# Order and size of the load bursts of a cached attention block, and half of its normalisation on another engine

## The chip, the cores and the metric

The kernel runs on one core of one Trainium2 chip. The metric is the device time of one execution in microseconds (us); lower is better. The kernel before took 459.73 us, the median of three runs (453.28 to 465.25).

A core has five engines that run their own instruction streams and meet only through semaphores: TensorE (matmuls; in the profile PE, with its weight loads as PEld), VectorE (DVE), ScalarE (ACT), GpSimd (POOL) and SyncE (SP), which here only issues transfers. Sixteen DMA engines carry out the transfers. Operands live in SBUF, matmul results in PSUM.

## The reference

```python
# x [8,112,640]; k_cache, v_cache [8,32,512,192]; wq [640,6144]; wo [6144,640]; all bf16
q = (x @ wq).reshape(B, Sq, H, Dh).transpose(0, 2, 1, 3)
scores = einsum("bhqd,bhkd->bhqk", q, k_cache) * Dh ** -0.5
p = softmax(scores, axis=-1)
o = einsum("bhqk,bhkd->bhqd", p, v_cache)
return o.transpose(0, 2, 1, 3).reshape(B, Sq, H * Dh) @ wo
```

Eight batches of 112 queries attend with 32 heads to 512 cached keys and values of width 192. Each cache holds 50.3 MB, each weight matrix 7.9 MB; all of it is read once.

## The kernel before, in words

**Units.** The work is cut into 64 units: a unit is one batch and a group of four heads (`u = 8 * g + b`). Eight groups follow one another, and within a group the eight batches. For a unit, TensorE computes the scores transposed (S, 96 small matmuls), ScalarE takes their exponential (`exp`, L932), TensorE multiplies by V (PV, 16 matmuls; a column of ones beside V gives the row sums), VectorE normalises (`do_NM`, L976 to L986), TensorE transposes the result (T, 6 matmuls), and ScalarE moves it to `oT` (`tevac`, L941). There is no maximum subtraction; the sums are instead checked for their range on GpSimd, and a flag would start a second, slower program that isn't run with these inputs.

**Projections.** The Q projection of a later group (`do_Q`) and the output projection of an earlier one (`do_O`) are cut into items, and `items_at[u]` spreads them over the units: mostly one Q item and two O items in a unit, in the third unit of a group four Q items and no O, in the fifth two Q items and two O. The items share two PSUM banks in turn, so an item waits for the eviction of the item before the last (`bank_free`).

**The order on each engine** is written out by hand. TensorE's pass u is S(u), PV(u-1), the first items, T(u-1), the other items. VectorE's pass is two of four transposes of K for unit u+2 (`do_KT`, L974, which also wait until S(u) has released their buffer), the normalisation of unit u-1, and the other two transposes among evictions of O items. ScalarE's pass is the four exponentials of unit u, the first Q evictions, `tevac(u-1)`, the other Q evictions.

**Normalisation.** `do_NM(u)` waits for PV(u); a reduction adds two partial sums a head (L979), a reciprocal follows (L982), a memset clears a column of PSUM for the next PV (L983), and one multiply of 112 x 768 values writes `os` (L986). T(u) waits for it (`vNM`). Heads 0 and 1 stand in one PSUM bank, heads 2 and 3 in the next.

**Loads.** K and V have four buffers each (`NK`, `NV`), filled by two halves of 384 KB; Wq and Wo have two buffers each, filled by pieces of 192 and 160 KB. SyncE issues all loads in one queue, in an order fixed when the program is built. A load waits on SyncE until its buffer is free: K for the transposes (`vKT`) of the unit four before, V for PV (`pPV`) of the unit four before, and everything behind it in the queue waits too.

**Periods.** TensorE's instructions are themselves fetched by DMA, in pieces of 16,384 bytes, as the records of the instruction queue show. `put` counts TensorE's instructions; at the first suitable matmul after each 256 of them, the first after 194 (`FIRST`), it raises `pF`. SyncE issues loads in bursts, one for each of the 69 periods so marked, each after a wait for `pF` (near L1125). Which loads belong to a burst is worked out from a nominal time: `place` is the unit that TensorE is in, plus a fraction. In the kernel before, each load has one number, the place at which it may be issued (K of u+3 at u, V of u+2 at u+0.5, and so on), the list is sorted by it, and a burst takes from its head whatever is at most 0.45 ahead of `place`, without a limit on bytes.

**The start.** Before the first period, SyncE issues the input, Wq of group 0, K(0), and after the first Q item K(1) and V(0).

## Time and profile before

| | |
|---|---|
| median of three runs | 459.73 us |
| the profiled execution's own time | 465.36 us |
| its span, first to last instruction | 463.7 us |
| mean granted TensorE clock | 0.971 |
| TensorE matmuls busy | 402.9 us, 87% |
| VectorE busy | 320.4 us, 69% |
| ScalarE busy | 220.1 us, 47% |
| data queue, share of 16 DMA engines | 80.0%, 118.71 MB |
| transposes of K, x256 | 870 ns each |
| exponentials, 448 wide, x256 | 550 ns each |
| multiply of the normalisation, x64 | 958 ns each |
| reciprocal, x64 | 178 ns each |
| K half-load, issue to landing, median | 5.2 us |
| V half-load, issue to landing, median | 5.0 us |

How to read it: the profile's page gives busy time by engine, forty slices of the span, and groups of instructions by line with what ended the idle time before them. Ends of matmuls are modelled, so a busy TensorE isn't necessarily one at its peak; its weight loads (PEld) show gaps more sharply. All TensorE instructions pass through a helper, so their lines are those of `matmul` (L800) and `transpose` (L803), and what they work on tells them apart: `qT,kt` is S, `vs,pT` is PV, `ident,os` is T, `xT,wqs` a Q item, `wos,oT` an O item. In the chain and the waits, `issue` is time in which the engine waited for nothing that the profile shows. The chain follows the work that ended last back from its end; the times there are when a step began and how long it held the chain.

### The profile page before, as it was taken

The page shows a single profiled execution, that of the slowest core. Times are in us where ns is not written, and L with a number is a line of the kernel's source. Part 1 is how long each engine was busy: PE and PEld are TensorE (multiplying, and loading weights), DVE is VectorE, ACT ScalarE, POOL GpSimd, SP SyncE. Part 2 cuts the span into 40 slices and gives each one's busy share as a digit, 9 for nine tenths or more (in the row PEclk, how much of TensorE's full clock was granted, in tenths as well). Part 3 has the DMA queues.
Part 4 walks back from the last instruction along what each step waited for, and adds up shares of the span by engine and source line. Part 5 has one row for each costly group of instructions (what it writes and reads, how often), then busy time and mean ns, then how long its engine had stood idle before and what let it go on. Part 6 is the DMA issues. An engine that isn't in the chain of part 4 may idle for free.

```text
span 463.7 us, 19950 instructions
## 1 busy us (share of the span) xinstructions
PE 402.9 (87%) x8749; PEld 303.9 (66%) x8749; DVE 320.4 (69%) x635; ACT 220.1 (47%) x421; POOL 43.1 (9%) x210
## 2 busy tenths in 40 slices
PE   8948997999889698999896999899878998897782
PEld 4626775777667576677674777677656776675561
DVE  2636786877777665877785688777757777887542
ACT  3625553555446433565453555464435653553420
POOL 1001001110011010110010111101101101111010
PEclk9979999999999988999998999999989999999998
DMA  8898998799988868879994899989878788987601
GB/s 281 279 331 259 307 307 267 246 316 300 308 271 270 252 177 296 271 222 308 306 319 151 251 310 324 291 247 296 274 233 255 237 263 280 284 245 238 216 31 35
DMA packets 100654, 120.04 MB, mean 259 GB/s; under 512 B 5585, under 2 KB 84177, under 8 KB 100561
## 3 DMA queue, kind: packets, MB, share of 16 engines
q1 hardware_dynamic: 100560, 118.71, 80.0%
q8 instruction: 70, 1.15, 1.0%
q14 instruction: 24, 0.19, 0.1%
HBM read 117.54 MB, written 1.15 MB: 256 GB/s over the span
## 4 chain that ended last, share of the span: by engine, by line
PE 48%; DMA 26%; DVE 12%; issue 9%; SPq 3%; ACT 1%; DVEq 0%
PE ps L800 43%; DMA kr<-in_k_cache_dram 26%; DVE kt L974 7%; PE ps L803 4%; DVE os L986 4%; SPq L1085 1%; SPq L1099 1%; SPq L1091 1%; ACT pT L932 1%; DVE rinv L982 1%; SPq L1078 0%; ACT oT L941 0%; DVE ps L983 0%; ACT xT L913 0%; DVE sm L979 0%
## 5 line engine op out<-in xcount | busy, mean ns | idle before, releaser
L974 DVE STREAM_TRANSPOSE kt<-kr 128x384 int32<-128x384 int32 x256 | 210.7, 870 | 95.5 <-DMA kr<-in_k_cache_dram 57.9
L932 ACT ACTIVATE pT<-ps 128x448 bf16<-128x448 f32 x256 | 118.5, 550 | 75.1 <-PE ps L800 75.1
L800 PE MATMUL ps<-vs,pT 128*128 128x193 bf16 x1024 | 100.3, 250 | 19.5 <-issue 15.9
L800 PE MATMUL ps<-wos,oT 128*128 128x320 bf16 x672 | 111.3, 304 | 3.5 <-issue 2.6
L800 PE MATMUL ps<-xT,wqs 128*128 128x448 bf16 x480 | 107.2, 361 | 1.8 <-ACT xT L913 0.8
L800 PEld LDWEIGHTS ps<-vs,pT 128*128 128x128 bf16 x1024 | 83.7, 98 | 27.2 <-issue 18.6
L800 PEld LDWEIGHTS ps<-qT,kt 32*128 32x128 bf16 x6144 | 77.7, 93 | 18.9 <-issue 14.8
L800 PE MATMUL ps<-qT,kt 32*128 32x112 bf16 x6144 | 87.8, 209 | 0.7 <-ACT qT L924 0.7
L924 ACT ACTIVATE qT<-ps 128x448 bf16<-128x448 f32 x96 | 52.1, 544 | 73.2 <-PE ps L800 72.7
L941 ACT ACTIVATE oT<-ps 128x672 bf16<-128x672 bf16 x64 | 46.7, 730 | 80.4 <-PE ps L803 80.4
L800 PEld LDWEIGHTS ps<-wos,oT 128*128 128x128 bf16 x672 | 64.0, 99 | 31.3 <-issue 4.2
L800 PEld LDWEIGHTS ps<-xT,wqs 128*128 128x128 bf16 x480 | 56.8, 126 | 26.0 <-issue 3.3
L986 DVE TENSOR_TENSOR os<-ps,rinv 112x768 bf16<-112x768 f32 x64 | 61.3, 958 | 2.2
L803 PE MATMUL ps<-ident,os 112*128 112x112 bf16 x384 | 30.9, 218 | 26.3 <-DVE os L986 26.0
L1062 POOL TENSOR_SCALAR bad<-rinv 112x4 f32<-112x4 f32 x64 | 14.4, 225 | 399.3 <-DVE rinv L982 399.3
L803 PEld LDWEIGHTS ps<-ident,os 112*128 112x128 bf16 x384 | 21.3, 100 | 44.0 <-DVE os L986 42.6
L1000 DVE TENSOR_TENSOR acc<-ps,acc 128x320 f32<-128x320 f32 x84 | 39.9, 475 | 2.4 <-PE ps L800 2.2
L979 DVE TENSOR_REDUCE sm<-ps 112x4 f32<-112x8 f32 x64 | 10.1, 158 | 23.4 <-PE ps L800 23.4
L1063 POOL TENSOR_SCALAR bad<-rinv 112x4 f32<-112x4 f32 x64 | 14.3, 224 | 4.0
L982 DVE RECIPROCAL rinv<-sm 112x4 f32<-112x4 f32 x64 | 11.4, 178 | 3.4
L1065 POOL TENSOR_TENSOR cnt<-cnt,bad 112x8 f32<-112x8 f32 x64 | 12.8, 200 | 5.3
L1000 DVE TENSOR_TENSOR xs<-ps,acc 128x320 bf16<-128x320 f32 x14 | 6.3, 482 | 2.2 <-PE ps L800 2.2
(30 smaller groups left out, 30.9 us busy)
## 6 DMA issues: line engine op xcount, KB each, us to landing
kr<-in_k_cache_dram SPq DMA_DIRECT2D x128, 384.0 KB, 5.2
vs<-in_v_cache_dram SPq DMA_DIRECT2D x128, 384.0 KB, 5.0
wos<-in_wo_dram SPq DMA_DIRECT2D x48, 160.0 KB, 5.2
wqs<-in_wq_dram SPq DMA_DIRECT2D x35, 192.0 KB, 4.4
out_dram<-xs SPq DMA_DIRECT2D x7, 160.0 KB, 2.6
wqs<-in_wq_dram SPq DMA_DIRECT2D x1, 960.0 KB
xs<-in_x_dram SPq DMA_DIRECT2D x1, 640.0 KB, 4.3
xs<-in_x_dram SPq DMA_DIRECT2D x1, 480.0 KB, 7.9
```

The lines of the kernel that those rows point to most:

```text
L800: return put(lambda: pe.matmul(out, w, m, start=start, stop=stop, **kw), start and not stop, us)
L803: return put(lambda: pe.transpose(out, m, eye), first, 0.05)
L924: act.activation(qT[g % 2][:, c, HQ * h:HQ * (h + 1)], ps[:, bank(it), 0:HQ], ACTF.Copy).then_inc(aQ, 1)
L932: act.activation(pT[u % 2][:, a, :, 0:SQ], ps[:, a, 0:4 * SQ].rearrange("p (t q) -> p t q", t=4), ACTF.Exp, scale=scale).then_inc(aEX, 1)
L941: act.activation(oT[:, :, SQ * b:SQ * (b + 1)].rearrange("p (k c) q -> p k c q", k=2), src.rearrange("p k (c q) -> p k c q", c=3), ACTF.Co ...
L974: dve.transpose(dst, src).then_inc(vKT, 1)
L982: dve.reciprocal(rinv[:, u % 4, :], sm[:]).then_inc(vRC, 1)
L986: dve.tensor_tensor(os_[u % 2][:].rearrange("p (k e d) -> p k e d", k=2, e=2), pv[0:SQ, :, :, 1:1 + DH], rinv[:, u % 4, :].rearrange("p (k ...
L1000: ins = dve.tensor_tensor(ob[:, m, cs] if g == NG - 1 else acc[:, m, cs], src, acc[:, m, cs], op=ALU.add)
L1062: gp.tensor_scalar(bad[:, 0, :], rinv[:, u % 4, :], LO, None, op0=ALU.is_lt)
L1063: gp.tensor_scalar(bad[:, 1, :], rinv[:, u % 4, :], HI, None, op0=ALU.is_gt).then_inc(gB, 1)
L1065: gp.tensor_tensor(cnt[:], cnt[:], bad[:], op=ALU.add).then_inc(gC, 1)
```

## The change

It has three parts.

1. *Which loads a period's burst holds.* Each load now has two numbers, a due place and an earliest place, and a size. The list is sorted by due place (K of u at u-2, V of u at u+1.25, Wq of g at 8g-5.6, Wo of g at 8g+3.3). For each period the list is gone through in that order, and a load is taken if its earliest place is reached (K at u-5, V at u-2.6, Wq at 8g-13, Wo at 8g-6) and if it still fits into 1.8 MB (`BURST`); one that doesn't fit is passed over for smaller ones. Before the first period, K(1) and K(2) are issued, and V(0) no longer.
2. *Normalisation.* VectorE multiplies heads 0 and 1 only. ScalarE multiplies heads 2 and 3, with two activations of 112 x 192 that take the reciprocal as scale (`norm`), queued after the four exponentials of the pass and before its Q evictions. T waits for both (`aNM` is new), and `do_NM` also waits for `aNM` of the unit four before. The memset moves ahead of the reciprocal.
3. *Order on VectorE in passes 1 to 3.* The normalisation is queued ahead of the two transposes of K, not behind them.

```diff
-    FIRST = 194
+    FIRST, BURST = 194, 1800000
...
             def do_T(u):
                 wait(vNM, u + 1)
+                wait(aNM, u + 1)
...
+            def norm(u):
+                W(act, vRC, u + 1)
+                W(act, pT_, u - 1)
+                for e in range(2):
+                    ins = act.activation(os_[u % 2][:, DH * (2 + e):DH * (3 + e)], pv[0:SQ, 1, e, 1:1 + DH], ACTF.Copy,
+                                         scale=rinv[:, u % 4, 2 + e:3 + e])
+                ins.then_inc(aNM, 1)
...
                     for a in range(4):
                         exp(u, a)
+                if u > 0:
+                    norm(u - 1)
...
                 W(dve, gB, u - 3)
+                W(dve, aNM, u - 3)
                 dve.tensor_reduce(sm[:].rearrange("p (k e) -> p k e", k=2), pv[0:SQ, :, :, 0:RW:RW - 1],
                                   axis=mybir.AxisListType.X, op=ALU.add).then_inc(vSM, 1)
                 W(dve, vSM, u + 1)
+                dve.memset(pv[:, :, :, RW - 1:RW], 0.0)
                 dve.reciprocal(rinv[:, u % 4, :], sm[:]).then_inc(vRC, 1)
-                dve.memset(pv[:, :, :, RW - 1:RW], 0.0)
                 W(dve, pT_, u - 1)
                 W(dve, vRC, u + 1)
-                dve.tensor_tensor(os_[u % 2][:].rearrange("p (k e d) -> p k e d", k=2, e=2), pv[0:SQ, :, :, 1:1 + DH],
-                                  rinv[:, u % 4, :].rearrange("p (k e) -> p k e", k=2)[:, :, :, None].broadcast_to(
-                                      [SQ, 2, 2, DH]), op=ALU.mult).then_inc(vNM, 1)
+                dve.tensor_tensor(os_[u % 2][:, 0:2 * DH].rearrange("p (e d) -> p e d", e=2), pv[0:SQ, 0, :, 1:1 + DH],
+                                  rinv[:, u % 4, 0:2, None].broadcast_to([SQ, 2, DH]), op=ALU.mult).then_inc(vNM, 1)
...
+                if 0 < u < 4:
+                    do_NM(u - 1)
                 for t in kts[:2]:
                     do_KT(u + 2, t)
-                if u > 0:
+                if u >= 4:
                     do_NM(u - 1)
...
             W(sp, pQ, 1)
-            load_k(1, 0)
-            load_k(1, 1)
-            load_v(0, 0)
-            load_v(0, 1)
...
+            for u in (1, 2):
+                load_k(u, 0)
+                load_k(u, 1)
+            KB, WQB, WOB = 393216, 196608, 163840
+            loads = [(u - 2.0, u - 5.0, KB, load_k, u, h) for u in range(3, NU) for h in range(2)]
+            loads += [(u + 1.25, u - 2.6, KB, load_v, u, h) for u in range(NU) for h in range(2)]
+            loads += [(8 * g - 5.6, 8 * g - 13.0, WQB, load_wq, g, c) for g in range(1, NG) for c in range(DC)]
+            loads += [(8 * g + 3.3, 8 * g - 6.0, WOB, load_wo, g, c) for g in range(NG) for c in range(6)]
             loads.sort(key=lambda w: w[0])
...
-                due = [w for w in loads if w[0] <= place + 0.45]
+                room, due = BURST, []
+                for w in loads:
+                    if w[1] <= place and w[2] <= room:
+                        due.append(w)
+                        room -= w[2]
                 if due:
                     sp.wait_ge(pF, n + 1)
-                for _, fn, p0, p1 in due:
-                    fn(p0, p1)
-                loads = loads[len(due):]
+                for w in due:
+                    w[3](*w[4:])
+                    loads.remove(w)
```

## The prediction

> **What bounds the kernel now.** I read the chain that ended last, then the waits, then timelines of single loops. Below, "loop u" is TensorE's pass from the scores S(u) to S(u+1): S(u), PV(u-1), one or two projection items, the transposes T(u-1), the other items. A "period" is one of the 69 stretches of 256 TensorE instructions; each begins with the signal pF on which SyncE issues one burst of loads.

> The chain, shares first, then one stretch of it (start, duration, what):

> ```profile
> PE 48%; DMA 26%; DVE 12%; issue 9%; SPq 3%; ACT 1%; DVEq 0%
> ```
> ```profile
> 115.03 5.56 DMA kr<-in_k_cache_dram
> 120.66 0.68 issue
> 121.34 0.84 DVE kt L974
> 122.52 0.97 DVE os L986
> 123.54 0.47 PE ps L803 x6
> ```

> A late K load holds VectorE's transposes of K, these hold the normalisation queued behind them, and that holds T on TensorE. The waits from 150 us to the end (who waited for whom: total us, times, longest):

> ```profile
> PEld ps L800 <- issue: 31.4, 58, 3.7
> DVE kt L974 <- DMA kr<-in_k_cache_dram: 29.9, 19, 2.8
> PEld ps L803 <- DVE os L986: 25.7, 37, 2.4
> ```

> The weight loads of TensorE in two neighbouring loops (start, busy, ..., idle before):

> ```profile
> 123.54 0.31 PEld L803 LDWEIGHTS ps<-ident,os 112*128 112x128 bf16 x6 [1.81 <-DVE os L986]
> ...
> 129.26 0.31 PEld L803 LDWEIGHTS ps<-ident,os 112*128 112x128 bf16 x6 [0.27 <-DVE os L986]
> ```

> So T waits for the normalisation in every ordinary loop: 1.81 us when K is late, 0.27 us when it isn't. Of the 25.7 us, 37 x 0.27 = 10.0 is this standing wait and 15.7 is late K. Where it appears, an undisturbed loop lasts 5.74 us (6.8 with two or four projections of Q).

> The third loss is a wait for nothing the profile shows:

> ```profile
> 73.41 0.28 PEld L800 LDWEIGHTS ps<-vs,pT 128*128 128x128 bf16 x4
> 76.79 0.96 PEld L800 LDWEIGHTS ps<-vs,pT 128*128 128x128 bf16 x12 [3.10 <-issue]
> ```

> It ends three or four matmuls ahead of a period's start, some 1.3 us after a 16,384-byte transfer on the instruction queue has landed: TensorE has run out of instructions because their fetch stood among data. Of the 31.4 us, 58 waits contain about 36 short ones of 0.26; some 22 us are long stalls, in the periods that begin outside S (loops 20-24, 33-37, 44-50, 59-62).

> [...] In this trace, with the queue near empty, the first 384 KB half-load of a burst lands 3.7 us after its period began, and each further half 1.1-1.2 us later, a Wq piece 0.5, a Wo piece 0.45; I use these. [...]

> **The change, part by part.** Sums are against the profiled execution's span, 463.7 us (465.36 with what lies around it, 1.2% above the median 459.73).

> *Normalisation.* [...] ScalarE gets two activations of 192[...]. They start when the reciprocal is ready, 3.45 us into an undisturbed loop (the memset of 0.06 us that moves ahead of the reciprocal partly fills its wait); ScalarE's four exponentials end at 3.24, so they aren't late. [...] T can start at 4.3 instead of 4.52, and TensorE itself is ready at 4.28. Gain at most 0.27 - 0.04 = 0.23 a loop. Queued behind the pair on ScalarE are a Q eviction and the eviction of T; [...] its bank is wanted after T, at 4.75: level, and a loss of 0.1 a loop is the bad end. 37 loops x 0.23 = 8.5 after 150 us, where most such loops are; some of these loops will wait for V or a fetch instead. I take **-6** (-8.5 to +4). The new wait of T on ScalarE adds nothing else; nothing but TensorE's next items stands behind it. POOL's range check reads the same reciprocal and has 400 us of idle time.

> *K earlier.* K(16), say, is still issued in loop 13, but leads its burst (before: half a V and often a Wq piece stood ahead, 1.2-1.7 us), and from loop 20 on it is up to two loops early. It lands 4.0-5.1 us after its period's start and is wanted 6.4 or more after. Late K after 150 us: 15.7; two or three remain: **-13** (-16 to -9).

> *Start, loops 0 to 11.* This is the price. V(0) loses its place ahead of the first period, and bursts are capped at 1.77 MB (first one before: 3.74). Replaying diff and period starts gives each burst's content; landing offsets as above give TensorE's wait. V(3) comes second in the period that starts with S(4) itself: its second half lands 3.7 + 1.1 + 1.1 = 5.9 us on, PV(3) is due 1.0 us on, wait 4.9. Likewise V(4) 4.6; V(5), whose period starts one item before S(6), 3.75; V(6) 2.45; V(7) 0.75; V(8) 0.7; V(9) 0.25. Before them V(0) 1.2, Wq of group 1 2.6 (three pieces arrive in the loop that needs them), V(2) 2.7, Wo of group 0 0.5. Sum 24.4. While TensorE waits, pF waits too, so DMA idles and nothing catches up. The kernel before loses 11.9 in the same stretch (S(12) at 99.2 against 87.3 from undisturbed loops), mainly late K(3), K(4) and one fetch stall; all of this goes, since normalisation now precedes the transposes in loops 1-3 and K(3) lands at 20.6, not 28.2. Net **+13** (+9 if waits overlap better, +20 if bursts land 1 us later, as some do).

> *Loops 12 to 19.* Bursts now read K, K, V, V: V(u) lands 3.7 + 3 x 1.15 = 7.2-7.4 us after a period that starts with S(u), and PV(u) is due 6.05 to 6.75 us after it. Waits: 2.0 in loop 12 (a Wo piece leads), 0.4 in the long loop 13, about 1.0 in each of five more, and 0.8 for a late Wo piece in loop 11: 8.2, against 3.4 of late K there before. **+5** (+1 to +9). From loop 21 V leads its burst or comes a loop earlier; one wait of 0.3-1.3 at PV(19), margins of 0.1-1 us for V(22) to V(31): **+2** (0 to +6).

> *Instruction fetches.* The cap is near the mean (113 MB in 67 bursts, 1.69), so it evens out the 1.93 MB bursts of periods within S, and raises those in short periods: 7.1 MB instead of 5.8 in periods 20-23, 8.6 instead of 7.4 in 33-37. A stall ends about 2.6 us after the fetch begins, and a fetch waits for what was queued. A 1.77 MB burst is down 7.5 us after its start, short periods are 4.4-5.7 us long: two of them just about cover 7.5 + 2.6. I take **-3** of the 22, for bursts that no longer carry over (-12 to +8: 1.2 MB more per short stretch at 300 GB/s is 4 us each). Last loops: K(63), late before, now comes early, **-1** (-3 to 0).

> Sum: -6 -13 +13 +5 +2 -3 -1 = -3: span 460.7, execution 462.4; scaled by 459.73/465.36, **456.8**; I say 456.

> **The rivals.** (A) *Even bursts free the fetches.* For it: between 80 and 150 us, periods with bursts of up to 1.93 MB ran without one. Against: stalls came even after bursts of 1.18 MB (253.0 us). Fetch -14, normalisation -7, K -14.5, start +12, loops 12-19 +4, V +1, end -2: -20.5, scaled **440**. (B) *V takes K's place, slower.* The place is PV(u-1) waiting for vs on TensorE, in loops 2-9, 12-18 and on to 33. Price: start +20, loops 12-19 +9, twelve loops at 0.7 = +8, K -13, normalisation -3 since V hides it, fetch -3, end -1: +17, scaled **476**. It decides from the point where a burst's second V half lands over 8 us after its period began, instead of 7.4; the burst at 253.6 took 9.4. Against it: most K-led bursts (77.1, 340.9) had V down by 7.0-7.6. (C) *Nothing net arrives earlier*: the cap is the mean, K is early only where it wasn't late: 460.

> **How the numbers follow.** Forecast 0.43, A 0.28, B 0.24, C 0.05. Two per cent, 450.5 and 468.9, is about what this kernel's runs (453 to 465) tell from no change. Faster by that is A and the low end of the forecast, 0.36; slower is B, 0.24; 0.40 between. The bounds above, taken together, give the forecast 445 to 468; reaching into A and B, the range is 438 to 476.

> **What would show it.** S(12) begins near 112 us (before: 99.2), with waits of 4-5 us before PV in loops 4 and 5 that end with a V load. In loops 12-18 such waits of about 1 us. VectorE's waits for K fall from 29.9 us after 150 to under 8. T's wait in undisturbed loops falls from 0.27 to about 0.05; loops last 5.5. Long issue stalls after 150 stay at 15-22 us in the same four stretches. I am wrong if the start loses nothing (V lands much sooner in an otherwise empty queue), if the fetch stalls vanish, or if V waits run on past loop 20.

## The result, and the profile after

The changed kernel takes **536.33 us** (median of four runs, 529.93 to 538.58) against 460.25 us before: the ratio is 1.166, 95% interval 1.124 to 1.207. The forecast was 456 us, no change. The profiled execution took 534.49 us, its span 532.2. Times below are medians of all executions; ratios and intervals use only those within 1.5% of a kernel's fastest, and none is given where too few are. Stretches are read from one profiled execution of each kernel. That of the kernel before (465.36) is the slowest of its own, some 5 us above the median, so a difference of stretches is uncertain by about as much. By the starts of the scores:

| stretch | before | forecast change | after | measured change |
|---|---|---|---|---|
| S(0) to S(12) | 83.7 us | +13 | 125.5 us | +41.8 |
| S(12) to S(20) | 51.2 | +5 | 60.0 | +8.8 |
| S(20) to S(62) | 285.9 | -20 (-6 -13 +2 -3) | 305.3 | +19.4 |
| S(62) to the end | 27.3 | -1 | 25.7 | -1.6 |

The pages have, below their tables of busy time, the clock granted to TensorE in 40 slices of the span (9 is 90% or more). First before, then after, with the chain after that ended last:

```profile
PEclk9979999999999988999998999999989999999998
```
```profile
PEclk9988777878998989799999899999988999987898
...
PE 77%; issue 14%; ACT 4%; DMA 2%; SPq 1%; DVE 0%; DVEq 0%
```

DMA has left the chain (26% before, 2% now), and VectorE with it (12%, now 0): K is no longer late. "Issue" has grown from 9 to 14%, and in slices 5 to 7 and 9 the clock is below eight tenths. The waits from 150 us to the end, as before (total us, times, longest):

```profile
PEld ps L800 <- issue: 68.8, 101, 4.1
PE ps L800 <- issue: 43.6, 23, 3.9
...
PE ps L800 <- ACT pT L933: 9.8, 5, 2.7
```

VectorE's waits for K (29.9 us before) are gone in this stretch, T's for the normalisation have fallen from 25.7 to 1.1 us, and the issue waits have doubled from 31.4 us. In the start, TensorE waits for V where the forecast put it. Loop 4, matmuls (start, busy, what, idle before):

```profile
48.96 1.36 PE L800 MATMUL ps<-qT,kt 32*128 32x112 bf16 x96
55.63 2.75 PE L800 MATMUL ps<-vs,pT 128*128 128x193 bf16 x16 [5.32 <-issue]
58.17 2.07 PE L800 MATMUL ps<-xT,wqs 128*128 128x448 bf16 x5
60.04 1.47 PE L800 MATMUL ps<-wos,oT 128*128 128x320 bf16 x6
```

The gap of 5.3 us was foreseen (4.9). What follows it was not: the five matmuls of the Q item take 2.07 us, where undisturbed loops show 1.11. The same 14 us in both kernels, after first, then before (stretch, length, busy PE, PEld, DVE, ACT, POOL, granted clock, DMA share, GB/s):

```profile
49.00:63.00 14.00, 8.68 (x139) 6.39 (x139) 5.21 (x12) 3.86 (x8) 0.65 (x3) 0.76 0.41 128
```
```profile
49.00:63.00 14.00, 14.00 (x293) 10.81 (x291) 11.37 (x23) 8.34 (x17) 1.30 (x6) 1.00 0.95 301
```

Later, a kind of stall appears that the kernel before hasn't got, within the scores. Weight loads of loop 33:

```profile
294.41 1.19 PEld L800 LDWEIGHTS ps<-qT,kt 32*128 32x128 bf16 x93 [0.26 <-issue]
298.99 0.10 PEld L800 LDWEIGHTS ps<-qT,kt 32*128 32x128 bf16 x3 [3.39 <-issue]
...
303.80 0.43 PEld L803 LDWEIGHTS ps<-ident,os 112*128 112x128 bf16 x6
```

T (303.80) waits no longer. But the scores stop 3.39 us short of three matmuls. Counted over TensorE's instructions, every such stall stands at number 193 or 194 of a block of 256 and ends 1.2 to 1.6 us after a 16,384-byte transfer of the instruction queue has landed. There are sixteen ahead of scores, 37.6 us in all; the kernel before has none.

**Late fetches.** I count a period's instruction fetch as late where it starts over 4 us after the period began; 67 of the 69 periods have a burst, and only these are counted. Before: 8 late, all in periods that begin outside the scores. After: 21, and 11 of them are all those periods that begin in the scores with 18 or fewer score matmuls left. The 21 fetches start 4.1 to 8.2 us into their periods; in the 11, most or all of the burst has moved by then (in the period from 215.72 us, 1.76 of its 1.77 MB).

### The profile page after: what moved, and what is told of

Its sections match the earlier page's. It is cut to its first block, busy times and chain, and to the rows that moved or that the text cites. A ratio compares the mean times of both kernels' runs of the same rounds, so it can differ in the third digit from the quotient of the medians.

```text
span 532.2 us, 20204 instructions
## 1 busy us (share of the span) xinstructions
PE 425.9 (80%) x8749; PEld 324.2 (61%) x8749; DVE 296.3 (56%) x635; ACT 261.6 (49%) x549; POOL 43.2 (8%) x210
## 3 DMA queue, kind: packets, MB, share of 16 engines
q8 instruction: 70, 1.15, 0.9%
HBM read 117.54 MB, written 1.15 MB: 223 GB/s over the span
## 4 chain that ended last, share of the span: by engine, by line
PE 77%; issue 14%; ACT 4%; DMA 2%; SPq 1%; DVE 0%; DVEq 0%
PE ps L800 73%; ACT pT L933 4%; PE ps L803 4%; DMA xs<-in_x_dram 2%; DMA wqs<-in_wq_dram 0%; SPq L1091 0%; ACT oT L950 0%; DVE kt L985 0%; SPq L1104 0%; ACT qT L925 0%; ACT os L940 0%; SPq L1117 0%; DVE xs L1011 0%; SPq L1085 0%; DVE rinv L995 0%
## 5 line engine op out<-in xcount | busy, mean ns | idle before, releaser
L800 PE MATMUL ps<-vs,pT 128*128 128x193 bf16 x1024 | 114.9, 272 | 51.9 <-issue 34.0
L800 PEld LDWEIGHTS ps<-vs,pT 128*128 128x128 bf16 x1024 | 95.4, 107 | 61.4 <-issue 36.7
L800 PE MATMUL ps<-qT,kt 32*128 32x112 bf16 x6144 | 91.4, 209 | 38.4 <-issue 37.7
L800 PE MATMUL ps<-xT,wqs 128*128 128x448 bf16 x480 | 115.3, 381 | 3.9 <-DMA wqs<-in_wq_dram 2.6
L800 PE MATMUL ps<-wos,oT 128*128 128x320 bf16 x672 | 114.1, 309 | 3.2 <-issue 2.2
L800 PEld LDWEIGHTS ps<-qT,kt 32*128 32x128 bf16 x6144 | 78.5, 93 | 58.3 <-issue 56.4
L800 PEld LDWEIGHTS ps<-wos,oT 128*128 128x128 bf16 x672 | 65.0, 101 | 35.8 <-issue 8.2
L940 ACT ACTIVATE os<-ps,rinv 112x192 bf16<-112x192 f32 x128 | 46.8, 416 | 79.8 <-DVE rinv L995 79.7
L800 PEld LDWEIGHTS ps<-xT,wqs 128*128 128x128 bf16 x480 | 58.8, 129 | 33.5 <-issue 10.0
L998 DVE TENSOR_TENSOR os<-ps,rinv 112x384 bf16<-112x384 f32 x64 | 35.7, 558 | 6.5
L803 PE MATMUL ps<-ident,os 112*128 112x112 bf16 x384 | 29.6, 212 | 0.6 <-ACT os L940 0.5
L803 PEld LDWEIGHTS ps<-ident,os 112*128 112x128 bf16 x384 | 25.2, 97 | 6.9 <-DVE os L998 1.1
```

The lines of the kernel that those rows point to most:

```text
L800: return put(lambda: pe.matmul(out, w, m, start=start, stop=stop, **kw), start and not stop, us)
L803: return put(lambda: pe.transpose(out, m, eye), first, 0.05)
L940: ins = act.activation(os_[u % 2][:, DH * (2 + e):DH * (3 + e)], pv[0:SQ, 1, e, 1:1 + DH], ACTF.Copy, scale=rinv[:, u % 4, 2 + e:3 + e])
L998: dve.tensor_tensor(os_[u % 2][:, 0:2 * DH].rearrange("p (e d) -> p e d", e=2), pv[0:SQ, 0, :, 1:1 + DH], rinv[:, u % 4, 0:2, None].broadc ...
```

## The experiments

The theory to begin with: the loads did it all. V comes too late at the start, a fetch that is asked for at the same moment as a burst lands behind it, and the idle gaps lower the clock.

**Parts 2 and 3 alone: the loads of before, the split normalisation.**

```diff
-            loads = [(u - 2.0, u - 5.0, KB, load_k, u, h) for u in range(3, NU) for h in range(2)]
+            loads = [(0.0, load_k, 2, 0), (0.0, load_k, 2, 1), (0.3, load_v, 1, 0), (0.3, load_v, 1, 1)]
...
```

> The changed kernel with the loads of the kernel before: only the split normalisation and the new VectorE order of loops 1 to 3 remain. Theory (the loads alone lost the time: V comes too late at the start, instruction fetches end up behind whole bursts, and TensorE's clock falls in the idle gaps that follow): about 455 us, between 448 and 463, S(12) within 2 us of the 99 us of the kernel before. Rival (ScalarE's two normalisation instructions in each loop hold up the pass that makes the items' outputs free, and so cost the time): over 480 us, with idle TensorE time ended by ScalarE.

Measured 497.17 us, ratio 1.089 (1.079 to 1.098). The theory falls: with the old loads the new stall is there, 16 times ahead of scores (36.1 us), and 22 fetches are late. Nor is it quite the rival's idle time behind ScalarE; it is issue.

**Part 1 alone: the new loads, the normalisation of before.**

```diff
-                wait(aNM, u + 1)
...
-            def norm(u):
...
```

> The changed kernel with the normalisation of the kernel before (four heads in one VectorE instruction); the new loads remain. Theory (loads): 525 to 545 us, S(12) at 140 us or a little later, the half-clock stretches of the changed kernel still there. Rival (normalisation): below 485 us.

Measured 488.09 us, 1.071 (1.061 to 1.080): neither. S(12) begins at 131.9 us; no stall ahead of scores, 3 late fetches. From S(20) to S(62) this kernel takes 267.1 us, 18.8 less than the kernel before. The two halves of the change lose 38 and 29 us by themselves, in different places.

**The burst later in its period.**

```diff
-    FIRST, BURST = 194, 1800000
+    FIRST, BURST = 226, 1800000
```

> The changed kernel with each burst's signal sent 32 TensorE instructions later in its period (FIRST 226 in place of 194), so that the instruction fetch of the period has had time to be asked for before the burst enters the queues. Theory (a fetch asked for at the same moment as a burst of 1.77 MB often lands behind all of it): the issue stalls of TensorE over 2 us after 150 us mostly go, from some 20 to fewer than 6, and the time falls by 20 to 45 us, to about 500; the late V of the start stays or grows a little, since V is asked for some 0.9 us later. Rival (the size of the bursts itself, or their data rate, holds up the fetches wherever they are asked for): the stalls stay and the time stays within 10 us of 536.

Measured 549.03 us, 1.191 (1.173 to 1.209): no gain over the changed kernel. 18 fetches are still late, among them again all 11 in the scores. So fetch and burst aren't simply asked for at the same moment, one just ahead of the other.

**The start of the kernel before.**

```diff
-            for u in (1, 2):
-                load_k(u, 0)
-                load_k(u, 1)
+            load_k(1, 0)
+            load_k(1, 1)
+            load_v(0, 0)
+            load_v(0, 1)
...
-                room, due = BURST, []
+                room, due = {0: 3800000, 1: 2600000}.get(n, BURST), []
```

> The changed kernel with a start like the one before: K(1) and V(0) ahead of the first period, and bursts of up to 3.8 MB in the first period and 2.6 MB in the second, 1.8 MB after that. Theory (the late V of loops 1 to 7 opens idle gaps, and these also lower the granted clock): S(12) at 105 us or before in place of 141, and about 495 us in all, the later fetch stalls being as they were. Rival (the start loses its time to the order of VectorE or to the fetches, not to V): S(12) stays over 125 us and the time over 520.

Measured 490.37 us, 1.074 (1.063 to 1.084). S(12) begins at 110.3 us, 31 earlier; what is missing to 105 is stalls of the new kind in loops 9 to 11 (6.5 us). S(12) to S(20) takes 47.4 us instead of 60.0, without a gap: with more data at the start, V is in time there too.

**The new theory** comes from what the first two runs tell apart: the new stall goes with the split normalisation, and what that adds to TensorE is one wait. In the traces of both kernels 408 of TensorE's weight loads carry one wait and none carries two; what a matmul waits for beyond that stands in a separate wait instruction ahead of it (254 of these on TensorE before, 318 after, one more for each of the 64 T). The first `wait` in the code stays with the matmul: the 64 T carry vNM, the 64 added instructions wait for aNM. The theory is that a separate wait holds TensorE's instruction stream, and with it the request for the next block; the traces show when a wait instruction is recorded, not what it holds. It fits the later signal too: in the 11 score periods of the changed kernel T's separate wait is recorded only 3.1 to 4.5 us in, and even the signal sent later came ahead of it in all 11.

**T on one wait, all else as changed.**

```diff
-                wait(vNM, u + 1)
-                wait(aNM, u + 1)
+                wait(nm, 2 * (u + 1))
...
-                ins.then_inc(aNM, 1)
+                ins.then_inc(nm, 1)
```

> The changed kernel with T waiting on one semaphore that both halves of the normalisation raise (T waits for the value 2(u+1)), in place of one semaphore each. TensorE's program loses the 64 separate wait instructions that stood ahead of T. Theory (a separate wait instruction holds TensorE's instruction stream until it is met, so the next block of 256 instructions is asked for too late, behind a burst): the sixteen issue stalls ahead of the scores, 37.6 us in the changed kernel, go, and the time falls from 536 to 480 to 495 us, the late V of the start being as it was. Rival (the two instructions on ScalarE are themselves what is slow, or the new loads hold up the fetches): over 520 us.

Measured 487.09 us (478.97 to 490.72). No stall ahead of scores, 3 late fetches, and the wait for issue after 150 us falls from 68.8 us:

```profile
PEld ps L800 <- issue: 37.0, 72, 3.5
```

The extra wait cost 49 us. What is left of the loss lies before S(20).

**The loads of before, the split normalisation, one wait** (the same edit on the first experiment).

> The loads of the kernel before, the split normalisation of the changed one, and T waiting on one semaphore that both halves raise. Theory (the separate wait was all that was wrong with the split): 445 to 460 us, somewhat under the kernel before. Rival (ScalarE's share costs time of its own): 470 to 497.

Measured 453.11 us, 0.984 (0.976 to 0.993): the split, with the new order of VectorE's passes 1 to 3, gains 6.7 us, little but clear of no change; ScalarE's share costs nothing that shows. The waits for issue after 150 us, first with two waits ahead of T, then with one:

```profile
PEld ps L800 <- issue: 62.4, 84, 4.1
```
```profile
PEld ps L800 <- issue: 25.9, 56, 3.4
```

**One more wait and nothing else, in both orders.** Two runs of the kernel before, T also waiting on the long-met vI:

```diff
+                wait(vI, 1)
                 wait(vNM, u + 1)
```

> The kernel before with one thing added: T also waits on vI, which was met at the start. The order of the two waits in the code puts the wait for the normalisation (vNM) into a separate wait instruction ahead of T, and the met one (vI) into T's first instruction. Nothing else moves. Theory (held stream): issue stalls ahead of the scores appear as in the changed kernel, some 30 to 37 us of them, and the time is 485 to 500 us. Rival (64 more instructions only shift where the blocks of 256 end, or the loss is that of ScalarE's work): within 3 per cent of the kernel before, or no different from its partner with the waits the other way round.

```diff
                 wait(vNM, u + 1)
+                wait(vI, 1)
```

> The same added wait as in its partner, in the other order: the separate wait instruction ahead of T is for vI, long met, and T's first instruction carries the wait for the normalisation, as in the kernel before. The count of instructions and the ends of the blocks are those of its partner. Theory (held stream): 455 to 470 us, with no more than 10 us of issue stalls ahead of the scores. Rival (it is the 64 instructions, or the shifted block ends): the same time as its partner, 485 to 500.

Measured 506.40 us, 1.100 (1.091 to 1.108), with vNM in the separate instruction, and 493.90 us, 1.062 (1.050 to 1.074), with vI in it. The wait for issue after 150 us, in that order:

```profile
PEld ps L800 <- issue: 64.8, 91, 4.3
```
```profile
PEld ps L800 <- issue: 58.2, 79, 4.3
```

The first is as expected: one wait and no other work makes the whole loss of the split. The second isn't: a met wait costs 34 us as well. An unmet one costs 12 more, so "held until met" is the smaller part; a separate wait instruction counts by being there. How a met one does it, the trace shows only in part, in the times at which it records wait instructions. A met wait ahead of T is recorded 17 matmuls (median) ahead of T's first; with vNM in the separate instruction it is recorded only when T is next, 0.1 us ahead. In the kernel before, in the period from 169.58 us (eight score matmuls left), the wait of the O ahead of T is recorded 0.53 us into the period, the fetch starts at 1.08, the burst's first data at 1.58, and between this O and T stands no wait instruction. With the met wait added, in the period from 349.00 us (four left), that O's wait is recorded at 0.69 and the added one at 1.66; data start at 1.55, the fetch at 6.89. So in this period the stream passes the added wait when the burst is already moving, and the fetch comes behind it. That the request stands behind just this wait is not shown.

Are the shifted block ends to blame? The position decides nothing by itself:

| kernels | separate waits | late, of periods with 18 or fewer score matmuls left | other late | median us |
|---|---|---|---|---|
| before | 254 | 0 of 8 | 8 | 460 |
| new loads alone | 254 | 0 of 8 | 3 | 488 |
| split, one wait | 254 | 0 of 8 | 7 | 453 |
| changed, one wait | 254 | 0 of 8 | 3 | 487 |
| changed | 318 | 11 of 11 | 10 | 536 |
| split, two waits | 318 | 11 of 11 | 11 | 497 |
| before, vNM ahead | 318 | 11 of 11 | 11 | 506 |
| before, vI ahead | 318 | 10 of 11 | 12 | 494 |

**Taking separate waits away.** If each counts, the kernel before has too many. O waits on aT although PV of the same loop has waited for as much:

```diff
-                wait(aT, 8 * g + last_unit(m) + 1)
+                if g == NG - 1 and m == MT - 1:
+                    wait(aT, 8 * g + last_unit(m) + 1)
```

> The kernel before without the wait of the output projections O on aT where PV of the same loop has waited for as much already (all but the last two O). About a hundred separate wait instructions of TensorE go; nothing else moves but the block ends, by as much. Theory (each separate wait instruction in its way shortens the lead of TensorE's instruction stream, and so delays the request for the next block): the long issue stalls, some 22 us after 150 us, mostly go, and the time falls by 8 to 20 us, to 440 to 452. Rival (only waits that aren't met hold the stream; these are always met): within 4 us of the kernel before.

Measured 441.44 us (434.83 to 445.59) against 457.99 (453.34 to 460.61). 152 separate waits are left, one fetch is late instead of eight, and the wait for issue after 150 us falls from 31.4 to 11.0 us. The expectation had one thing wrong. What stood in the separate instruction was not the met wait on aT, which rode on the matmul, but the second one, for a free bank, which rides there now. In the kernel before few of these 112 waits were held: 8 are recorded within 0.05 us of the eviction that they wait for.

**Both repairs** (the start's diff and that of the one wait, together), and then both with this third edit of O:

> Both repairs together: the changed kernel with the start of the kernel before (K(1) and V(0) ahead of the first period, bursts of up to 3.8 and 2.6 MB in the first two periods) and T waiting on one semaphore. Theory (the late V of the start and the separate wait ahead of T were the two losses, and they add): S(0) to S(12) takes 84 to 88 us, S(12) to S(20) 47 to 49, S(20) to S(62) 266 to 271, in all 440 to 450 us, faster than the kernel before and than the split normalisation with the loads before (453). Rival (a start with more data brings the late fetches back, or the gain of the new loads was only that of a late start): 453 to 465.

Measured 436.72 us, 0.954 (0.950 to 0.958): 79.6, 47.4 and 265.6 us for the three stretches, 20.3 less than before in the third. The start repairs its own loss and the one wait the other.

> The two repairs together, and O's redundant waits on aT left out as well. Theory (every separate wait counts): 8 to 20 us under the same kernel with these waits, about 430. Rival (only unmet waits count): no different from it.

Measured **408.57 us, 0.893 (0.888 to 0.897)**: better than both kernels, and by more than expected. It doesn't tell met waits from unmet ones: with both repairs alone, 50 of O's 112 separate waits are recorded within 0.05 us of their eviction, so these were held. Clock and chain of its page, and its wait for issue from 140 us to the end:

```profile
PEclk9999999999999999999999999999999999999998
...
PE 90%; DMA 3%; SPq 2%; issue 1%; ACT 1%; DVE 1%; DVEq 0%
```
```profile
PEld ps L800 <- issue: 13.2, 44, 1.0
```

S(20) to S(62) takes 243.5 us, with 0.9 us of gaps. Without the new loads, the faster loop waits for K more (60.4 us, up from 57.9); with them it doesn't, so the loads now earn what they were made for.

**What a gap costs beside its length.** The kernel before, run once (496.94 us), with VectorE held by dummy writes ahead of five normalisations:

```diff
+                for _ in range({26: 24, 40: 24, 54: 24, 29: 6, 43: 6}.get(u, 0)):
+                    W(dve, vP, paused[0])
+                    dve.memset(zero[:], 0.0).then_inc(vP, 1)
...
```

> The kernel before with VectorE held by dummy writes ahead of the normalisation in five loops: 24 writes in loops 27, 41 and 55 (an idle gap of some 8 to 10 us on TensorE ahead of T), 6 writes in loops 30 and 44 (some 2 us). It measures what an idle gap costs beside its own length. Theory (idle time lowers TensorE's clock for a while): after each long gap a window of about 3.4 us with matmuls at twice their usual time, costing 1.5 to 3.5 us more than the gap; after the short gaps none. Rival (the half-clock windows of the changed kernel come from its load or its place in time, not from idleness): matmuls at their usual time after every gap.

Matmuls in an undisturbed loop, after the first long gap, and after a short one:

```profile
188.90 0.47 PE L803 MATMUL ps<-ident,os 112*128 112x112 bf16 x6 [0.87 <-DVE os L990]
189.20 0.98 PE L800 MATMUL ps<-wos,oT 128*128 128x320 bf16 x6
190.12 1.36 PE L800 MATMUL ps<-qT,kt 32*128 32x112 bf16 x96
...
217.89 0.74 PE L803 MATMUL ps<-ident,os 112*128 112x112 bf16 x6 [9.16 <-DVE os L990]
218.42 1.81 PE L800 MATMUL ps<-wos,oT 128*128 128x320 bf16 x6
220.16 1.88 PE L800 MATMUL ps<-qT,kt 32*128 32x112 bf16 x96
...
239.98 0.47 PE L803 MATMUL ps<-ident,os 112*128 112x112 bf16 x6 [2.28 <-DVE os L990]
240.29 0.98 PE L800 MATMUL ps<-wos,oT 128*128 128x320 bf16 x6
```

After 9.2 us of idleness the projection takes 1.81 us instead of 0.98; after 2.3 us, 0.98. From the starts of the operations, the three long gaps cost 1.6, 2.7 and 2.8 us beyond their length, the two short ones nothing. The granted clock by stretch:

```profile
208.00:211.00 3.00, 0.73 (x6) 0.29 (x3) 2.04 (x9) 0.49 (x1) 0.43 (x2) 1.00 0.87 284
211.00:214.00 3.00, 0.00 (x0) 0.00 (x0) 2.05 (x8) 0.00 (x0) 0.00 (x0) 0.51 0.46 159
...
218.50:220.00 1.50, 1.50 (x8) 0.68 (x5) 1.19 (x3) 0.73 (x1) 0.00 (x0) 0.50 0.00 0
...
221.50:223.00 1.50, 1.50 (x60) 1.41 (x45) 0.75 (x2) 0.92 (x3) 0.00 (x0) 1.00 0.25 46
```

It falls to half 2.4 us into this gap, 5.1 us into the other two, and returns 3.4, 5.8 and 6.2 us after work resumes, 10.2 us at half speed each time. But a gap need not be long: in the kernel before, five of the six stalls of 2.1 to 3.6 us after 50 us came with 3.4 us at half speed, from 0.5 us before to 1.3 us after their end (the Q item after the stall that ends at 162.53 us takes 2.07 us), the sixth, of 2.9 us, did not. That the two short gaps here cost nothing is thus no rule. In the changed kernel loops 4 to 7 have gaps of 3.9 to 5.6 us each, and each comes with 3.4 to 6.8 us at half speed: the work of loops 0 to 11, gaps taken out, lasts 86.5 us instead of 71.6.

## Why the prediction was wrong

**The step that failed** is a sentence in the part on the normalisation: "The new wait of T on ScalarE adds nothing else; nothing but TensorE's next items stands behind it." I asked who is queued behind the wait, and not what form it takes. In the form it took, with two semaphores, it is a separate instruction in TensorE's stream, 64 times over. Its price is the difference between the changed kernel and the same with one wait: 46.4 us of span, 35.0 of it between S(20) and S(62), where the term for fetches said -3 with +8 as its bad end.

**The second is the start term, +13, measured +32.5** with one wait. Its mechanism was right, the size off. The waits came where they were replayed (with one wait, loop 4: 5.4 for 4.9; loop 5: 5.0 for 4.6; loop 2, Wq: 2.1 for 2.6), but gaps are 20.8 us more than before instead of 12.5, mainly since V(5) to V(9) came later than replayed (13.0 us of waits for 7.9); and the sum left out the clock: the same work took 11.7 us more, with the clock at half speed in places. Loops 12 to 19 were sized right (+7.0 for +5).

**Right**, though the total hid it: the normalisation at -6 (-6.7 measured, together with the new order of passes 1 to 3). ScalarE's two operations took 416 ns each, VectorE's 558 for two heads (958 for four before); the lengths on which T's start at 4.3 us rested were the author's estimate, which no trace of the kernel before shows. And the agreement is partly luck: an undisturbed loop gained 0.09 us, not 0.23 (5.65 us for 5.74). T's waits after 150 us did fall from 25.7 to 10.2 us, those behind a late K among them. K earlier: DMA left the chain. All terms from S(20) to S(62) together, -20: -15.6 with one wait, -20.3 with the start repaired as well, both against a profile of the kernel before that is some 5 us slow.

**Of the rivals**, B named the right side and place, V waits in loops 2 to 9, and priced the start at +20 for the measured +32.5; its V waits from loop 20 on came to 7.4 us with one wait (loops 20 to 30), near its +8 and over the forecast's +2, and are gone with the start repaired. Its point of decision doesn't hold: with one wait the second halves of V landed 6.3 to 6.7 us into their periods in loops 4 to 6, not over 8, and the start lost all the same. A, even bursts that free the fetches, holds in part where the added wait is gone: 3 late fetches for 8 with the new loads alone, but 7 with the start repaired. Of the signs named, S(12) near 112 was missed (141.2, and 132.0 with one wait), V waits in loops 12 to 18 were 1.7 to 2.8 us, every second loop, and issue stalls doubled in place of staying.

**What stays open**: what triggers the request for the next block. The runs show that with separate waits ahead of T the fetch comes late, and where, not how. One period doesn't fit a request that waits for T: in the changed kernel, in the one from 509.72 us, with 17 score matmuls left but no burst, the fetch starts 1.76 us in, though T's wait is recorded only at 3.09.

## What to carry to other kernels

Count the waits of an instruction before adding one: here a second became an instruction of its own in the engine's stream, and 64 of these cost 44 to 49 us where the split that they guard gained 6.7, in a program that is fetched in blocks of 16 KB beside bursts of up to 1.8 MB. Let both producers raise one semaphore (where, as here, neither can get a unit ahead of the other), drop waits that an earlier wait implies (17 us here), and give the matmul itself the wait that is met last (493.90 us against 506.40). And price an idle gap of TensorE, of 9 us in the test, at up to 3 us more than its length; here even a gap of 2.1 us came with 3.4 us at half speed.
